# Two transformer layers on one core: Mish products on VectorE, rounding on ScalarE, w2 two feature tiles behind w1

## Chip, cores and metric

The kernel runs on one core of one Trainium2 chip. The metric is the device time of one execution in microseconds (us). The kernel before takes 3567.12 us (median of 3 runs, 3566.23 to 3567.72).

## What is computed

Two layers, each an attention block and a dense block with residuals, both with the same weights in both layers. `x` is 2048 tokens by 512; there are 32 heads of 16; `w1` is 512 x 1792, `w2` is 1792 x 512. The dense block is what the change touches:

```python
h = layernorm(x) @ w1 + b1
sp = log1p(exp(-abs(h))) + where(h > 0, h, 0)
x = x + (h * tanh(sp)) @ w2          # Mish, then the second matrix
```

## The kernel before

**Numbers and splits.** A float32 matmul is made of three matmuls of a faster type (fp32r): an operand is split into a rounded high part and a low part (the rest), and high x high, high x low and low x high are summed in PSUM (`mm3`, lines 176 to 181). So the Mish result is needed twice: `ah`, its rounding, and `al = act - ah`.

**Stages.** For each of the two layers: normalize and multiply by `wqkv`; attention (some 1250 us); `wo`; then the dense block (`mlp`, line 687), some 340 us each time. In the trace's time the dense blocks lie at about 1445 to 1795 us and 3219 to 3560 us.

**The dense block.** Tokens come in 4 chunks `c` of 512, features in 14 tiles `f` of 128. A step of the loop (line 746) is one `(c, f)`. `hid(c, f)` issues 12 matmuls (w1, output tile `h`) and the Mish chain; then the hooks of that step run; then `outp` of the step LAG = 3 back issues 12 matmuls (w2, output tiles `mo`) that add up over all 14 `f` in PSUM: 8 with `ah` as the stationary operand (high and low part of w2 in turn for each of 4 token tiles), then 4 with `al`. After `f` = 13 four additions (line 739) put the result onto the residual `x2`, and free the `mo` banks for the next chunk.

**The Mish chain of one tile** (lines 701 to 717, all 128 x 512): ScalarE `hb` = h + b1; VectorE `he` = min(hb, 10); ScalarE exp; VectorE `he` = (e + 2) e; ScalarE `hr`: a logarithm and an exponential that make the reciprocal; GpSimd `hb` = hb x he (line 708); VectorE `ah` = hb x hr, rounded as it is written (711 or 715); GpSimd the same product again, unrounded (712 or 716); VectorE `al` = hb - ah (713 or 717). The last two tiles of the last layer have VectorE in GpSimd's place. Tiles `hb`, `ah` and `al` have 2 buffers each, `he` and `hr` have 1. For chunks 1 to 3 `ah` and `al` are written in a permuted token order (views `mixed` and `grouped`, runs of 32).

**What else stands in the block.** The first chunk's block also carries the last quarter of the `wo` projection: `outs[3].parts` (hook at step 2) multiplies `num` by `rec` on VectorE (line 655), rounds `oh` on ScalarE (661) and takes `ol` on VectorE (662), all 128 x 2048; four hooks named `quarter` at steps 5, 6, 7 and 8 issue 12 matmuls each (`wo`). The hooks load the later tiles of w1 and w2 (1 MB each, SP queue). `spread` hooks six parts of the next chunk's normalization onto successive steps: statistics, scaling (278), 32 x 32 transposes (283), writes to DRAM in turned order (286), reading back (291), then split on ScalarE and VectorE (294, 295).

**What sets the order.** Matmuls of a layer are chained in program order. Everything else is placed by a list scheduler at build time, by its own estimate of time with the program order as priority; so an engine's order can differ from the order of the text. At run time every engine, and the SP queue, works strictly in the order so fixed. SBUF tiles of 1 MB share 22 slots (`blk`), and a load waits until the slot's last user is done.

Of the kernel before, what the change touches and what calls it, by code (L numbers as in the profile page):

```python
# [9 lines left out]
F32 = mybir.dt.float32  # L10
F32R = mybir.dt.float32r
BF16 = mybir.dt.bfloat16
AF = mybir.ActivationFunctionType
ALU = mybir.AluOpType
# [4 lines left out]
P = 128  # L19
S, D, H, DH, F = 2048, 512, 32, 16, 1792  # L20
NCH = 4
# [3 lines left out]
FT = F // P  # L25
# [21 lines left out]
GSTEPS = NCH * NKT  # L47
STEPS = NG * GSTEPS
HEADS = STEPS * HG
LAG = 3  # L50
MAX_M = (6, 3, 7)
T_BUFS = {"he": 1, "hr": 1}
NBLK = 22
# [15 lines left out]
def kernel(ctx: ExitStack, tc: tile.TileContext, x, wqkv, wo, w1, b1, w2, out):  # L69
    nc = tc.nc  # L70
    x = x[0]
# [37 lines left out]
    def pbank(tag, name):  # L109
        if tag == "s":  # L110
            return banks["s"].tile([P, 512], F32, tag=tag, name=name, bufs=3)
        return ps.tile([P, 512], F32, tag=tag, name=name, bufs=1)

    def t512(tag, name, dt=F32):
        return tmp.tile([P, 512], dt, tag=tag, name=name, bufs=T_BUFS.get(tag, 2))
# [60 lines left out]
    def mm3(acc, pairs, first=True, last=True, pe=lambda ins: ins):  # L176
        n = len(pairs)
        for i, (ah, al, bh, bl) in enumerate(pairs):
            pe(nc.tensor.matmul(acc, ah, bh, start=first and i == 0, stop=False))  # L179
            pe(nc.tensor.matmul(acc, ah, bl, start=False, stop=False))  # L180
            pe(nc.tensor.matmul(acc, al, bh, start=False, stop=last and i == n - 1))  # L181
# [78 lines left out]
    def mixed(t):  # L260
        return t.rearrange("p (j g r) -> p g j r", j=2, r=TR)

    def grouped(t):
        return t.rearrange("p (g j r) -> p g j r", j=2, r=TR)

    def norm_blocks(src, nm, got, key):
        rs, mv = statistics(src, nm)
        yield
        th = b8([P, KT, CW], F32R, f"th{nm}")
        tl = b8([P, KT, CW], F32R, f"tl{nm}")  # L270
        got[key] = (th, tl)
        raw = tl.bitcast(F32)
        turned = dram.tile([D, CW], F32, name=f"nt{nm}")
        for h in range(2):
            xn = tmp.tile([P, 2, D], F32, tag="raw", name=f"xn{nm}{h}", bufs=3)
            for j in range(2):
                t = h + 2 * j
                nc.vector.tensor_scalar(
                    xn[:, j], src[:, t], mv[:, t, 0:1], rs[:, t : t + 1], op0=ALU.subtract, op1=ALU.mult
                )  # L280
            y = tmp.tile([P, D // TR, 2, TR], F32, tag="raw", name=f"y{nm}{h}", bufs=3)
            for j in range(2):
                nc.vector.transpose(y[:, :, j], xn[:, j].rearrange("p (b r) -> p b r", r=TR))
            for a in range(P // TR):
                n0 = h * CW // 2 + a * 2 * TR
                nc.sync.dma_start(
                    turned[:, n0 : n0 + 2 * TR].rearrange("(b q) n -> q b n", q=TR),
                    y[ts(a, TR)].rearrange("q b j r -> q b (j r)"),
                )
            yield  # L290
        nc.sync.dma_start(raw, turned.rearrange("(k p) n -> p k n", p=P))
        yield
        for k in range(KT):
            nc.scalar.activation(th[:, k], raw[:, k], AF.Copy)
            nc.vector.tensor_tensor(tl[:, k], raw[:, k], th[:, k].bitcast(F32), op=ALU.subtract)
            if k % 2:
                yield

    def spread(hooks, c, f0, src, nm, got, key):
        parts = norm_blocks(src, nm, got, key)  # L300
        for i in range(6):
            hooks.setdefault((c, f0 + i), []).append(lambda: next(parts, None))

    class Attention:
# [9 lines left out]
        def pe(self, ins):  # L314
            if self.chained:
                if self.last is not None:
                    tc.add_manual_dep(
                        ins.ins,
                        self.last.ins.name,
                        mybir.DependencyInfo(mybir.DependencyClass.NoSync, mybir.DependencyReason.DATA),  # L320
                        reason="issue order",
                    )
                self.last = ins
# [363 lines left out]
    def mlp(l, x2s, w1t, w2t, tts, dst, hooks, pe):  # L687
        acts, obs = {}, {}

        def hid(c, f):  # L690
            th, tl = tts[c]
            w = w1t[f // 2]
            acc = pbank("s", f"h{l}{c}{f}")
            mm3(
                acc,
                [(w[:, 0, k, ts(f % 2, P)], w[:, 1, k, ts(f % 2, P)], th[:, k, :], tl[:, k, :]) for k in range(KT)],
                pe=pe,
            )
            nm = f"{l}{c}{f}"
            hb, e, r = t512("f", "hb" + nm), t512("he", "he" + nm), t512("hr", "hr" + nm)  # L700
            nc.scalar.activation(hb, acc, AF.Identity, bias=b1t[:, f : f + 1])  # L701
            nc.vector.tensor_scalar(e, hb, HCLAMP, None, op0=ALU.min)  # L702
            nc.scalar.activation(e, e, AF.Exp)  # L703
            nc.vector.scalar_tensor_tensor(e, e, 2.0, e, op0=ALU.add, op1=ALU.mult)  # L704
            nc.scalar.activation(r, e, AF.Ln, bias=1.0, scale=0.5)  # L705
            nc.scalar.activation(r, r, AF.Exp, bias=lnhalf, scale=-1.0)
            mul = nc.vector if (l, c) == (1, NCH - 1) and f >= FT - 2 else nc.gpsimd
            mul.tensor_tensor(hb, hb, e, op=ALU.mult)  # L708
            ah, al = t512("ah", "ah" + nm, F32R), t512("al", "al" + nm, F32R)
            if c:  # L710
                nc.vector.tensor_tensor(mixed(ah), grouped(hb), grouped(r), op=ALU.mult)
                mul.tensor_tensor(hb, hb, r, op=ALU.mult)  # L712
                nc.vector.tensor_tensor(mixed(al), grouped(hb), mixed(ah.bitcast(F32)), op=ALU.subtract)  # L713
            else:
                nc.vector.tensor_tensor(ah, hb, r, op=ALU.mult)
                mul.tensor_tensor(hb, hb, r, op=ALU.mult)
                nc.vector.tensor_tensor(al, hb, ah.bitcast(F32), op=ALU.subtract)
            acts[c, f] = (ah, al)

        def outp(c, f):  # L720
            if f == 0:
                obs[c] = [ps.tile([P, 2, 512], F32, tag="mx", name=f"mo{l}{c}{i}") for i in range(2)]
            ah, al = acts.pop((c, f))
            w = w2t[f // 2]
            for act, parts in ((ah, (0, 1)), (al, (0,))):
                for t in range(NCH):
                    for part in parts:
                        pe(
                            nc.tensor.matmul(  # L729
                                obs[c][t // 2][:, t % 2],  # L730
                                act[:, ts(t, P)],
                                w[:, part, f % 2],
                                start=f == part == 0 and act is ah,
                                stop=f == FT - 1 and act is al,
                            )
                        )
            if f == FT - 1:
                for t in range(NCH):
                    nc.vector.tensor_tensor(x2s[c][:, t], obs[c][t // 2][:, t % 2], x2s[c][:, t], op=ALU.add)
                    if l == 1 and c == NCH - 1:  # L740
                        nc.sync.dma_start(dst[c * CW + t * P : c * CW + (t + 1) * P, :], x2s[c][:, t])
                if l == 0 or c < NCH - 1:
                    nc.sync.dma_start(dst[ts(c, CW), :].rearrange("(t p) d -> p t d", p=P), x2s[c])

        seq = [(c, f) for c in range(NCH) for f in range(FT)]
        for i in range(len(seq) + LAG):
            if i < len(seq):
                c, f = seq[i]
                hid(c, f)
                for fn in hooks.get((c, f), []):  # L750
                    fn()
            if i >= LAG:
                outp(*seq[i - LAG])

# [47 lines left out]
    for l in range(2):  # L802
# [19 lines left out]
        wot, w1t, w2t, x2s, tts = [], [], [], [], {}  # L822
# [13 lines left out]
        hooks = {}  # L836
# [46 lines left out]
        hooks = {}  # L883

        def on(f, fn, c=0):
            hooks.setdefault((c, f), []).append(fn)
# [5 lines left out]
            for _ in range(KT):  # L892
                next(rest)

        for f in range(5, 9):
            on(f, quarter)
        for i, (f1, f2) in enumerate(((0, 0), (2, 2), (4, 6), (7, 8)), 3):
            on(f1, lambda i=i: load_w1(i))
            on(f2, lambda i=i: load_w2(i - 1))
        on(9, lambda: load_w2(6))  # L900
        for c in range(NCH - 1):
            spread(hooks, c, 5 if c else 0, x2s[c + 1], f"m{l}{c + 1}", tts, c + 1)
        wts, tt = {}, {}
        if l == 0:
            last = NCH - 1
# [34 lines left out]
```

## Time and profile before

| | |
|---|---|
| median of 3 runs | 3567.12 us |
| the profiled execution | 3567.44 us |
| its span in the trace | 3565.7 us |
| TensorE (PE) busy | 3524.6 us, 99% |
| VectorE (DVE) busy | 3028.7 us, 85% |
| ScalarE (ACT) busy | 2519.1 us, 71% |
| GpSimd (POOL) busy | 571.0 us, 16% |
| granted TensorE clock, mean | 0.996 |

The span is what the engines' instructions cover; 1.7 us of the execution lie around it. A row of the view by lines reads: line, engine, operation, output tile <- input tiles, shapes, count | busy us, mean ns of one | idle time of the engine just before, and what ended it. A row of the view of time reads: start us, duration us, engine, line, operation, tiles [idle before <- releaser]. A row of waits reads: who waited, for whom, us in total, times, longest. A matmul's row is longer than its share of the time, since matmuls overlap.

### The profile page before, as it was taken

What the parts mean: (1) busy time and instruction counts of PE and PEld (TensorE: products, weight loads), DVE (VectorE), ACT (ScalarE), POOL (GpSimd) and SP (SyncE); (2) the same over time, 40 slices, a digit from 0 to 9 for tenths busy, and PEclk for the clock granted to TensorE, in tenths of its full rate; (3) what the DMA queues carried; (4) which work ended last, traced back from release to release, by engine and by line L of the source; (5) the groups of instructions that cost most, each with busy time, mean ns of one, the idle gap of its engine ahead of it and who ended that gap; (6) DMA issues with size and microseconds to landing.
All of it is one profiled execution on the core that took longest, in us unless ns stands there. A gap on an engine that the chain in (4) does not pass through costs nothing.

```text
span 3565.7 us, 69085 instructions
## 1 busy us (share of the span) xinstructions
PE 3524.6 (99%) x28572; PEld 1931.1 (54%) x28572; DVE 3028.7 (85%) x3052; ACT 2519.1 (71%) x3401; POOL 571.0 (16%) x612
## 2 busy tenths in 40 slices
PE   9999999999999999999999999999999999999999
PEld 7644444444444444777776444444444444447777
DVE  6799999999999994766756999999999999937666
ACT  3288888888888887344422888888888888863444
POOL 3101001000000002455520000000000000024554
PEclk9999999999999999999999999999999999999999
DMA  7641322312222124620364211112121121256000
GB/s 249 225 90 50 79 56 64 62 61 59 66 60 47 52 69 78 224 68 24 107 219 145 47 38 41 35 29 47 29 46 28 41 38 50 61 94 223 36 12 24
DMA packets 182199, 273.99 MB, mean 77 GB/s; under 512 B 67508, under 2 KB 111476, under 8 KB 168060
## 3 DMA queue, kind: packets, MB, share of 16 engines
q1 hardware_dynamic: 154964, 192.91, 21.1%
q10 hardware_dynamic: 19176, 43.06, 3.5%
q0 software_dynamic: 7744, 33.60, 3.3%
q8 instruction: 224, 3.67, 0.4%
q14 instruction: 91, 0.75, 0.1%
HBM read 158.87 MB, written 109.58 MB: 75 GB/s over the span
## 4 chain that ended last, share of the span: by engine, by line
PE 89%; DVE 5%; POOL 2%; ACT 2%; issue 1%; DMA 1%; DVEq 0%; ACTq 0%; POOLq 0%
PE pv L457 30%; PE pm L383 17%; PE ss L441 13%; PE sp L431 9%; PE mo L729 6%; PE qk L179 2%; PE h L179 2%; PE h L181 2%; PE h L180 2%; PE qk L180 1%; PE qk L181 1%; POOL hb L712 1%; DVE al L713 1%; PE wo L179 1%; PE va L179 1%
## 5 line engine op out<-in xcount | busy, mean ns | idle before, releaser
L387 DVE TENSOR_REDUCE mxv<-pm 128x2 f32<-128x1024 f32 x2048 | 2385.3, 1219 | 138.1 <-PE pm L383 89.1
L432 ACT ACTIVATE p<-sp 128x1024 f32<-128x1024 f32 x1366 | 1395.7, 1022 | 18.9 <-PE sp L431 14.6
L457 PE MATMUL pv<-p,va 128*32 128x256 f32 (+2 forms) x16032 | 1167.0, 392 | 0.1
L383 PE MATMUL pm<-ks,qs 48*128 48x512 f32 x4096 | 1097.9, 447 | 0.2
L442 ACT ACTIVATE p<-ss 128x512 f32<-128x512 f32 x1364 | 814.6, 597 | 349.7 <-PE ss L441 272.6
L431 PE MATMUL sp<-qs,ks 50*128 50x512 f32 x2732 | 726.2, 446 | 0.3
L383 PEld LDWEIGHTS pm<-ks,qs 48*128 48x128 f32 x4096 | 451.4, 184 | 345.1 <-issue 177.4
L457 PEld LDWEIGHTS pv<-p,va 128*32 128x32 f32 x16032 | 368.1, 108 | 496.3 <-issue 418.7
L441 PE MATMUL ss<-qs,ks 50*128 50x512 f32 x1364 | 612.5, 449 | 0.0
L441 PEld LDWEIGHTS ss<-qs,ks 50*128 50x128 f32 x1364 | 252.3, 185 | 329.4 <-ACT p L442 225.4
L431 PEld LDWEIGHTS sp<-qs,ks 50*128 50x128 f32 x2732 | 261.6, 183 | 200.2 <-ACT p L432 118.3
L402 POOL CAST np<-nt 128x32 fp32r<-128x32 f32 x64 | 13.3, 208 | 2212.5 <-DVE nt L400 2174.5
L705 ACT ACTIVATE hr<-he 128x512 f32<-128x512 f32 x112 | 70.8, 632 | 215.0 <-POOL hb L712 128.3
L713 DVE TENSOR_TENSOR al<-hb,ah 128x512 fp32r<-128x512 f32 x84 | 122.6, 1459 | 72.4 <-POOL hb L712 70.0
L712 POOL TENSOR_TENSOR hb<-hb,hr 128x512 f32<-128x512 f32 x82 | 139.1, 1696 | 204.0 <-ACT he L703 139.7
L708 POOL TENSOR_TENSOR hb<-hb,he 128x512 f32<-128x512 f32 x110 | 148.7, 1351 | 58.5 <-DVE he L704 55.6
L173 ACT ACTIVATE pt<-qk 128x512 fp32r<-128x512 f32 x64 | 38.2, 597 | 142.2 <-PE qk L181 105.1
L703 ACT ACTIVATE he<-he 128x512 f32<-128x512 f32 x112 | 70.8, 632 | 82.1 <-DVE he L702 72.8
L702 DVE TENSOR_SCALAR he<-hb 128x512 f32<-128x512 f32 x112 | 52.6, 470 | 84.7 <-ACT hb L701 62.7
L701 ACT ACTIVATE hb<-h,b1t 128x512 f32<-128x512 f32 x112 | 76.9, 687 | 64.4 <-DVE al L713 28.4
L704 DVE SCALAR_TENSOR_TENSOR he<-he 128x512 f32<-128x512 f32 x112 | 82.0, 732 | 21.4 <-ACT he L703 14.0
L174 DVE TENSOR_TENSOR pt<-qk,pt 128x512 fp32r<-128x512 f32 x64 | 43.9, 685 | 50.5 <-ACT pt L173 48.3
(240 smaller groups left out, 3186.6 us busy)
## 6 DMA issues: line engine op xcount, KB each, us to landing
scr<-pt ACTq DMA_DIRECT2D x64, 512.0 KB
qs<-scr SPq DMA_DIRECT2D x174, 128.0 KB
ks<-scr SPq DMA_DIRECT2D x174, 128.0 KB
vscr<-v SPq DMA_DIRECT2D x32, 512.0 KB
va<-vscr SPq DMA_DIRECT2D x64, 256.0 KB
oscr<-ot SPq DMA_DIRECT2D x64, 256.0 KB
ww<-sw POOLq DMA_DIRECT2D x14, 1024.0 KB, 5.0
num<-oscr SPq DMA_DIRECT2D x64, 128.0 KB
```

Of the source, the lines that this page charges most:

```text
L179: pe(nc.tensor.matmul(acc, ah, bh, start=first and i == 0, stop=False))
L383: nc.tensor.matmul(pm[:, e], qs[u][rows, q0 : q0 + P], ks[u][rows, ts(n, 512)], start=True, stop=True)
L387: nc.vector.tensor_reduce(self.mxs[b][:, 2 * u : 2 * u + 2, qt, n], pm, axis=AX.X, op=ALU.max)
L431: self.pe(nc.tensor.matmul(sp[:, e], k, q, start=True, stop=True))
L432: nc.scalar.activation(self.pts[-1][:, 0:n], sp[:, 0:n], AF.Exp, scale=SCALE)
L441: self.pe(nc.tensor.matmul(sp, k, q, start=True, stop=True))
L442: nc.scalar.activation(self.pts[i // 3][:, 2], sp, AF.Exp, scale=SCALE)
L457: nc.tensor.matmul(self.accs[b][ts(h, VW), cols], self.va[b // NCH][:, kt, h, :], self.pts[j][:, e, cols], start=kt == 0 and q0 == 0, stop ...
L708: mul.tensor_tensor(hb, hb, e, op=ALU.mult)
L712: mul.tensor_tensor(hb, hb, r, op=ALU.mult)
L713: nc.vector.tensor_tensor(mixed(al), grouped(hb), mixed(ah.bitcast(F32)), op=ALU.subtract)
L729: nc.tensor.matmul(obs[c][t // 2][:, t % 2], act[:, ts(t, P)], w[:, part, f % 2], start=f == part == 0 and act is ah, stop=f == FT - 1 and ...
```

## The change

LAG goes from 3 to 2. Both Mish products are VectorE's, always; the product is taken once, and the rounding of `ah` is a ScalarE copy. Of each `outp` the matmuls with the high part of w2 come first for all four token tiles, then those with the low part, then `al`; for the last feature tile each token tile's three matmuls stand together. The four quarters are hooked at steps 6 to 9, and the next chunk's normalization, for chunk 1, at steps 7 to 12 in place of 0 to 5.

```diff
-LAG = 3
+LAG = 2
...
-            mul = nc.vector if (l, c) == (1, NCH - 1) and f >= FT - 2 else nc.gpsimd
-            mul.tensor_tensor(hb, hb, e, op=ALU.mult)
+            nc.vector.tensor_tensor(hb, hb, e, op=ALU.mult)
+            nc.vector.tensor_tensor(hb, hb, r, op=ALU.mult)
             ah, al = t512("ah", "ah" + nm, F32R), t512("al", "al" + nm, F32R)
-            if c:
-                nc.vector.tensor_tensor(mixed(ah), grouped(hb), grouped(r), op=ALU.mult)
-                mul.tensor_tensor(hb, hb, r, op=ALU.mult)
-                nc.vector.tensor_tensor(mixed(al), grouped(hb), mixed(ah.bitcast(F32)), op=ALU.subtract)
-            else:
-                nc.vector.tensor_tensor(ah, hb, r, op=ALU.mult)
-                mul.tensor_tensor(hb, hb, r, op=ALU.mult)
-                nc.vector.tensor_tensor(al, hb, ah.bitcast(F32), op=ALU.subtract)
+            high, low, full = (mixed(ah), mixed(al), grouped(hb)) if c else (ah, al, hb)
+            nc.scalar.activation(high, full, AF.Copy)
+            nc.vector.tensor_tensor(low, full, high.bitcast(F32), op=ALU.subtract)
             acts[c, f] = (ah, al)
...
-            for act, parts in ((ah, (0, 1)), (al, (0,))):
-                for t in range(NCH):
-                    for part in parts:
-                        pe(
...
+            terms = [[(t, act, part) for t in range(NCH)] for act, part in ((ah, 0), (ah, 1), (al, 0))]
+            turns = zip(*terms) if f == FT - 1 else [terms[0] + terms[1], terms[2]]
+            for t, act, part in (x for turn in turns for x in turn):
+                pe(
...
-        for f in range(5, 9):
+        for f in range(6, 10):
             on(f, quarter)
...
-            spread(hooks, c, 5 if c else 0, x2s[c + 1], f"m{l}{c + 1}", tts, c + 1)
+            spread(hooks, c, 5 if c else 7, x2s[c + 1], f"m{l}{c + 1}", tts, c + 1)
```

In the changed file the same lines lie up to five higher or lower: 707 and 708 are the products, 711 the copy, 712 `al`, 724 the w2 matmuls, 734 the additions; 701 to 706 keep their numbers.

More of the change, by code (lines that the diff above doesn't have):

```diff
@@ L724, in outp @@
             w = w2t[f // 2]
-            for act, parts in ((ah, (0, 1)), (al, (0,))):
-                for t in range(NCH):
-                    for part in parts:
-                        pe(
[L729 to L736, printed above, removed]
+            terms = [[(t, act, part) for t in range(NCH)] for act, part in ((ah, 0), (ah, 1), (al, 0))]
+            turns = zip(*terms) if f == FT - 1 else [terms[0] + terms[1], terms[2]]
+            for t, act, part in (x for turn in turns for x in turn):
+                pe(
+                    nc.tensor.matmul(
+                        obs[c][t // 2][:, t % 2],
+                        act[:, ts(t, P)],
+                        w[:, part, f % 2],
+                        start=f == part == 0 and act is ah,
+                        stop=f == FT - 1 and act is al,
+                    )
+                )
             if f == FT - 1:
```

## The prediction

> **What bounds the kernel now.** I read the page's busy shares first, then TensorE's waits in the two stretches that hold the dense blocks, then the clock in those stretches, then one tile's chain in order of time.
>
> ```profile
> PE 3524.6 (99%) x28572; PEld 1931.1 (54%) x28572; DVE 3028.7 (85%) x3052; ACT 2519.1 (71%) x3401; POOL 571.0 (16%) x612
> ```
>
> TensorE is busy 99% of the span, and the change takes no matmul away. So all that can be won is what TensorE waits, and what its clock loses by waiting. The changed program has the same instructions in the same order outside the dense blocks (on all engines; only names differ), so I look there alone. Waits from 1444.67 to 1800, then from 3218.9 to the end:
>
> ```profile
> PE wo L179 <- ACT oh L661: 6.5, 1, 6.5
> PE mo L729 <- DVE x L739: 6.2, 3, 4.3
> PE mo L729 <- DVE al L713: 1.6, 1, 1.6
> PE wo L181 <- DVE ol L662: 1.2, 1, 1.2
> PE mo L729 <- DVE al L717: 0.6, 2, 0.4
> ...
> PE wo L179 <- ACT oh L661: 6.5, 1, 6.5
> PE mo L729 <- DVE x L739: 3.4, 3, 2.1
> PE wo L181 <- DVE ol L662: 1.2, 1, 1.2
> PE mo L729 <- DVE al L717: 1.0, 2, 0.8
> ```
>
> 16.1 + 12.1 = 28.2 us of idle time in 15 waits. The clock, for the four stretches in which it was halved and one undisturbed stretch of 60 us (columns: stretch, length, busy us and count of PE, PEld, DVE, ACT, POOL, granted clock, DMA share, GB/s):
>
> ```profile
> 1472.10:1482.35 10.25, 6.79 (x15) 4.92 (x16) 8.38 (x11) 4.96 (x6) 5.06 (x3) 0.50 0.74 254
> 1639.36:1646.19 6.83, 5.84 (x14) 4.60 (x15) 6.33 (x15) 2.60 (x4) 3.08 (x3) 0.50 0.41 155
> 3247.04:3257.28 10.24, 7.05 (x16) 5.09 (x17) 8.37 (x11) 4.96 (x6) 5.32 (x3) 0.50 0.75 263
> 3414.29:3417.70 3.41, 3.41 (x9) 2.65 (x10) 2.13 (x4) 1.32 (x2) 0.67 (x1) 0.50 0.79 296
> 1560.00:1620.00 60.00, 60.00 (x261) 48.82 (x261) 41.52 (x59) 28.36 (x45) 31.59 (x22) 1.00 0.19 53
> ```
>
> Undisturbed, 261 matmuls take 60 us: 0.23 each, 2.77 a block of 12, 5.53 a step. At half clock TensorE worked 6.79 + 5.84 + 7.05 + 3.41 = 23.1 us, half of it lost: 11.5. A matmul's row lasts about 0.39 though the next starts after 0.23, so a wait also costs 0.16 more than the idle time shown: 15 x 0.16 = 2.4. **What waiting costs now: 28.2 + 11.5 + 2.4 = 42.1 us.** That is the ceiling, but for the tail.
>
> Why it waits, in one tile of the steady part:
>
> ```profile
> 1700.97 0.69 ACT L701 ACTIVATE hb<-h,b1t 128x512 f32<-128x512 f32 x1 [0.47 <-DVE al L713]
> 1701.77 0.43 DVE L702 TENSOR_SCALAR he<-hb 128x512 f32<-128x512 f32 x1 [0.89 <-ACT hb L701]
> 1702.23 0.63 ACT L703 ACTIVATE he<-he 128x512 f32<-128x512 f32 x1 [0.57 <-DVE he L702]
> 1702.89 0.69 DVE L704 SCALAR_TENSOR_TENSOR he<-he 128x512 f32<-128x512 f32 x1
> 1702.96 1.77 POOL L712 TENSOR_TENSOR hb<-hb,hr 128x512 f32<-128x512 f32 x1 [2.63 <-ACT he L703]
> 1704.77 0.63 ACT L705 ACTIVATE hr<-he 128x512 f32<-128x512 f32 x1 [1.91 <-POOL hb L712]
> 1705.44 0.73 ACT L706 ACTIVATE hr<-hr,lnhalf 128x512 f32<-128x512 f32 x1
> 1707.77 0.69 DVE L711 TENSOR_TENSOR ah<-hb,hr 128x512 fp32r<-128x512 f32 x1
> 1708.62 1.77 POOL L712 TENSOR_TENSOR hb<-hb,hr 128x512 f32<-128x512 f32 x1 [2.63 <-ACT he L703]
> 1710.43 1.77 DVE L713 TENSOR_TENSOR al<-hb,ah 128x512 fp32r<-128x512 f32 x1 [1.18 <-POOL hb L712]
> ```
>
> One tile takes 11.2 us from `hb` to the end of `al`, and the next tile's `hb` starts (row 1) when an `al` is done. The ring of `hb`, `hr`, GpSimd's product and `al` comes round in 5.66 us (that product at 1702.96 and 1708.62): longer than TensorE's step, so it loses a little each step and the additions on `x` come late at a chunk's end.
>
> **The change part by part.**
>
> Prices: the rows show, in turn, a VectorE product, the two kinds of `al`, and a ScalarE copy with rounding.
>
> ```profile
> L712 DVE TENSOR_TENSOR hb<-hb,hr 128x512 f32<-128x512 f32 x2 | 1.4, 687 | 0.0
> L717 DVE TENSOR_TENSOR al<-hb,ah x28: 645/690/1778, 1457.3 to 3322.0; 128x512 fp32r<-128x512 f32 x28
> L713 DVE TENSOR_TENSOR al<-hb,ah x84: 674/1768/1781, 1552.1 to 3557.0; 128x512 fp32r<-128x512 f32 x84
> L294 ACT ACTIVATE thm<-tlm x24: 613/617/632, 1485.2 to 3392.1; 128x512 fp32r<-128x512 f32 x24
> ```
>
> A product on VectorE is 0.69 (row 1). `al` is 0.69 or 1.77 (rows 2 and 3: smallest 0.65 and 0.67, largest 1.78); the long ones run beside a GpSimd product, and after the change GpSimd has none: 0.69. The copy is 0.62 (row 4, the same shape and types). So a step costs VectorE 0.43 + 0.69 + 0.69 + 0.69 + 0.69 = 3.19 us in place of 0.43 + 0.69 + 0.69 + 1.77 = 3.58, and ScalarE 0.69 + 0.63 + 0.63 + 0.73 + 0.62 = 3.30 in place of 2.68: both under 5.53. The chain is hb, min, exp, square, two reciprocal steps, product, copy, `al` = 0.69 + 0.43 + 0.63 + 0.69 + 0.63 + 0.73 + 0.69 + 0.62 + 0.69 = 5.80, with about 0.05 at each of 8 hand-overs 6.2 us. LAG 2 leaves four blocks, 11.1 us. So in the steady part TensorE does not wait, though the cover shrinks by one step. If the VectorE terms stayed at 1.77 the step would be 6.4: a rival below.
>
> The waits on the additions (9.6) and on `al` (3.2) go. The changed order has the additions in two pairs beside the last `outp`, whose token tiles now finish one by one: the first pair can end 2.7 us after that block begins, the second at 5.4 to 6.1; the next chunk's w2 block needs those banks at about 5.5 and 6.0. I leave 0.2 for each of 6 chunk changes: 1.2.
>
> Start of each dense block. This is where the shorter lag costs. The first chunk's start before, in order of time:
>
> ```profile
> 1447.60 0.69 ACT L701 ACTIVATE hb<-h,b1t 128x512 f32<-128x512 f32 x1 [8.29 <-PE h L181]
> 1451.61 0.69 DVE L704 SCALAR_TENSOR_TENSOR he<-he 128x512 f32<-128x512 f32 x1 [0.54 <-ACT he L703]
> 1452.84 0.39 PE L179 MATMUL h<-thm,w11l 128*128 128x512 f32 x1
> 1453.00 0.72 ACT L706 ACTIVATE hr<-hr,lnhalf 128x512 f32<-128x512 f32 x1
> 1454.93 1.82 DVE L278 TENSOR_SCALAR xnm<-x,mvm,rsm 128x512 f32<-128x512 f32 x2
> 1469.05 3.35 DVE L655 TENSOR_TENSOR num<-num,rec 128x2048 f32<-128x2048 f32 x1
> 1472.43 1.91 ACT L661 ACTIVATE oh<-num 128x2048 fp32r<-128x2048 f32 x1 [1.91 <-DVE num L655]
> 1474.45 2.28 DVE L662 TENSOR_TENSOR ol<-num,oh 128x2048 fp32r<-128x2048 f32 x1
> ```
>
> After the change the first w2 block stands at 1452.84, where the fourth `h` block stood (row 3). `hr` of tile 0 ends at 1453.72 (row 4); product and copy bring `ah` at 1455.2. Wait: 2.4. Its `al` stands behind two scalings and a 0.69: 1457.3, wait 0.2.
>
> Then the second wait. In layer 0's changed order VectorE and ScalarE do `num`, `oh` and `ol` before tile 3's product and copy. Walking the order with these prices: tile 3's `h` ends at 1461.2, its `hb` (behind tile 2's copy) at 1463.5, min at 1464.3, scalings to 1465.9, `num` (without GpSimd beside it I take 2.3, as `ol`) to 1468.2, `oh` to 1470.1, then square, transposes, product, `ol` to 1473.1, min of tile 4, product 1474.2, copy 1474.8. TensorE wants that `ah` at 1472.1: wait 2.8. So the 6.5 us in front of the first quarter do not vanish: part turns up one block earlier. The quarter itself, one step later, comes at about 1480, with `oh` and `ol` there: the 13.0 and 2.4 go. In layer 1 the order has tile 3's product and copy ahead of `ol`: the same walk gives 0.3 for `ah` and 0.8 for `al`.
>
> Clock after these waits. Idle times of 2.1 or more (the list above: 6.5, 4.3, 2.1) were followed by half clock, the 1.6 was not. The 2.8 I charge with one shortest stretch, 3.41 at half speed: 1.7; the two of 2.4 (2.2 idle) with half of that each: 0.9. The Trainium skill, "TensorE: Matmul & The Clock Gate", section "Why this matters for your kernels", names idle gaps of more than about 3 us as what drops the clock. By that these waits would cost no clock and the sum would be 3.5 us lower; this trace's 2.1 us did drop it, so I keep the charge.
>
> The next chunk's normalization. Its read-back now stands on the SP queue behind the last two w2 loads, and its slot is freed by the last quarter; ScalarE's split of it stands ahead of tile 10's reciprocal.
>
> ```profile
> 1475.64 0.38 SPq L291 DMA_DIRECT2D tlm<-ntm  x1
> 1485.15 2.20 ACT L294 ACTIVATE thm<-tlm 128x512 fp32r<-128x512 f32 x4 [3.87 <-DMA tlm<-ntm]
> ```
>
> Before, it also followed two 1 MB loads and ScalarE had it 9.5 us after its issue. Issued after the last quarter (call its end 0), it lands at about 10; the splits end at 13, VectorE's part at 15.6, tile 10's copy at 17.2; TensorE wants it at 6 blocks = 16.6. I charge 0.5 in each layer: 1.0. The other moves on that queue (w1 and w2 loads some 4 us earlier, transposed writes) have steps of cover. Between the layers I leave 0.3.
>
> The tail.
>
> ```profile
> 3559.75 2.48 DVE L739 TENSOR_TENSOR x<-mo,x 128x512 f32<-128x512 f32 x4 [2.11 <-PE mo L729]
> ```
>
> The four additions run after the matmuls; token by token only the last stays: 1.3 less. LAG 2 leaves two blocks, 5.5, for the last tile's `ah` of about 5.6, and `al` next: 0.3 more. Net 1.0 less.
>
> The reordering of the other w2 matmuls keeps their number and weight loads; the `al` blocks already change banks at every matmul and keep the pace. Nothing.
>
> **Sum**: remaining 2 x (2.4 + 0.2 + 0.9) + (2.8 + 1.7) + 1.1 + 1.2 + 1.0 + 0.3 = 15.1. Gain 42.1 - 15.1 + 1.0 = 28.0. From the profiled execution's 3567.4 (0.3 above the median): **3539.4 us**.
>
> **Rivals.**
> 1. *The waits move rather than go.* The walk through the first steps may be short: if the read-back lands 5 us later and the `oh` work delays tile 3 by as much in layer 1 as in layer 0, that adds 2 x (5 + 1.7) + (1.7 + 1.7) = 16.8: 3556. For it: ScalarE did wait 3.87 for that DMA. Against: the 9.5 us are measured behind the same two loads.
> 2. *The chain becomes the bound: slower.* VectorE's two-input products could run at 1.77, as `al` often does. Then a step is 0.43 + 0.69 + 3 x 1.77 = 6.4, 0.9 over TensorE's over 112 steps: +101 for the gain lost, about 3640. It decides from a mean of 1.47 for those three. Against: the 687 ns row, and an idle GpSimd. A milder form: strict in-order queues make one tile's round end before the next begins, 5.80 - 0.69 + hand-overs = 5.5 to 5.6; that would be as the old ring, slower only with an extra stop each step. The changed order has at most every second tile so bound in the steady part.
> 3. *The change moves the cover and gains only the chunk ends*: 9.6 + 3.2 + half-clock 4.6 = 17: 3550.
>
> **How the numbers follow.** Forecast (3531 to 3546) 0.68; rival 3 and rival 1 (3546 to 3560) 0.22; under 3531, if no clock falls and the start waits are shorter, 0.03; within 0.2% 0.02; slower, rival 2, 0.05. A measurement of this kernel can tell about 0.2%, 7 us. Range 3530 to 3554: the upper end takes in most of rivals 1 and 3. Faster 0.93, same 0.02, slower 0.05.
>
> **What would show it.** TensorE's waits: none on `oh`, `ol` or the additions above 0.3; a wait of about 2.4 on `ah` at both starts and 2.8 in layer 0 before tile 3's w2 block. `al` rows 0.69 throughout; the steady step 5.55. Wrong it is if VectorE's products show 1.7, if ScalarE waits long for the read-back, or if half-clock stretches stand at other places.

## Result and profile after

The changed kernel takes **3532.86 us** (median of 5 runs, 3531.69 to 3537.39) against 3567.12 before (5 runs, 3566.23 to 3567.79): a ratio of 0.9906, 95% interval 0.9891 to 0.9920. The profiled execution is the median one, 3532.86 us with a span of 3531.1: 34.6 us less than the profiled execution of before. The forecast was 3539.4, with 28.0 won.

First the busy shares on the page of the changed kernel:

```profile
PE 3512.9 (99%) x28572; PEld 1922.5 (54%) x28572; DVE 3002.7 (85%) x3160; ACT 2582.8 (73%) x3513; POOL 239.2 (7%) x392
```

TensorE still has 28572 matmuls and 99%. Its busy time shrank by 11.7 us, mostly matmuls that no longer run at half clock; the rest of the gain is idle time that went. What it still waits for in the two dense blocks, first layer, then second:

```profile
PE mo L724 <- ACT ah L711: 3.6, 2, 2.2
...
PE mo L724 <- ACT ah L711: 2.2, 1, 2.2
PE tpm L256 <- DVE xnm L210: 0.4, 1, 0.4
PE mo L724 <- DVE al L712: 0.3, 1, 0.3
```

28.2 us in 15 waits became 6.1 in 4 (`tpm` belongs to the stage before). Nothing waits for `oh`, `ol` or the additions on `x`. What is left are the first w2 block of each layer (2.2 each) and tile 3, in layer 0 on `ah` (1.4) and in layer 1 on `al` (0.3). The clock around both starts, and in the same undisturbed stretch as before:

```profile
1451.82:1455.23 3.41, 1.25 (x6) 0.72 (x5) 3.08 (x7) 2.50 (x4) 0.42 (x1) 1.00 1.03 239
1455.23:1458.65 3.42, 3.42 (x10) 2.65 (x9) 3.02 (x6) 2.65 (x5) 0.00 (x0) 0.50 1.14 164
...
3206.27:3209.68 3.41, 2.73 (x13) 1.92 (x11) 2.61 (x7) 2.52 (x5) 2.73 (x6) 1.00 1.03 241
3209.68:3213.09 3.41, 1.92 (x8) 1.62 (x9) 3.28 (x6) 2.12 (x5) 0.79 (x1) 1.00 1.07 237
...
1560.00:1620.00 60.00, 60.00 (x261) 48.77 (x260) 37.88 (x61) 38.33 (x61) 0.00 (x0) 1.00 0.10 25
```

One stretch at half clock is left, 3.42 us (row 2), where there were 30.7. In the undisturbed stretch (last row) TensorE's 261 matmuls take 60 us as before; VectorE went from 41.5 to 37.9 there, GpSimd from 31.6 to 0, ScalarE from 28.4 to 38.3.

The rows of `al` over both layers of the changed kernel; then VectorE's rows at the chunk end at which the additions came latest, in the kernel before and in the changed one:

```profile
L712 DVE TENSOR_TENSOR al<-hb,ah x112: 650/692/695, 1455.6 to 3523.1; 128x512 fp32r<-128x512 f32 x112
```

```profile
1634.62 1.77 DVE L713 TENSOR_TENSOR al<-hb,ah 128x512 fp32r<-128x512 f32 x1 [1.18 <-POOL hb L712]
1637.28 0.43 DVE L702 TENSOR_SCALAR he<-hb 128x512 f32<-128x512 f32 x1 [0.89 <-ACT hb L701]
1637.62 0.68 DVE L711 TENSOR_TENSOR ah<-hb,hr 128x512 fp32r<-128x512 f32 x1
1638.40 0.69 DVE L704 SCALAR_TENSOR_TENSOR he<-he 128x512 f32<-128x512 f32 x1
1639.01 2.48 DVE L739 TENSOR_TENSOR x<-mo,x 128x512 f32<-128x512 f32 x4
```

```profile
1621.47 1.28 DVE L734 TENSOR_TENSOR x<-mo,x 128x512 f32<-128x512 f32 x2
1622.67 0.68 DVE L704 SCALAR_TENSOR_TENSOR he<-he 128x512 f32<-128x512 f32 x1
1623.27 1.28 DVE L734 TENSOR_TENSOR x<-mo,x 128x512 f32<-128x512 f32 x2
```

Before, the additions stood on VectorE behind a whole round of the ring: `al` waits for GpSimd's product, `hb` waits for `al`, min waits for `hb`, and only then come the additions, 5.8 us after the chunk's last w2 block (TensorE's next block starts at 1633.18). Now they run inside and just behind the last w2 block (1619.42 to 1622.38), and TensorE's next w2 block starts at 1624.97 without a wait.

### The profile page after: what moved, and what is told of

It reads as the page before. It is cut to its first block, busy times and chain, and to the rows that moved or that the text cites. A ratio compares the mean times of both kernels' runs of the same rounds, so it can differ in the third digit from the quotient of the medians.

```text
span 3531.1 us, 68820 instructions
## 1 busy us (share of the span) xinstructions
PE 3512.9 (99%) x28572; PEld 1922.5 (54%) x28572; DVE 3002.7 (85%) x3160; ACT 2582.8 (73%) x3513; POOL 239.2 (7%) x392
## 4 chain that ended last, share of the span: by engine, by line
PE 96%; DVE 2%; DMA 1%; issue 1%; ACT 0%; POOL 0%; SPq 0%; DVEq 0%; ACTq 0%; POOLq 0%
PE pv L457 30%; PE pm L383 18%; PE ss L441 13%; PE sp L431 10%; PE mo L724 8%; PE h L179 3%; PE h L181 3%; PE h L180 3%; PE qk L179 2%; PE qk L180 1%; PE qk L181 1%; PE wo L179 1%; PE va L179 1%; PE wo L181 1%; PE wo L180 1%
## 5 line engine op out<-in xcount | busy, mean ns | idle before, releaser
L705 ACT ACTIVATE hr<-he 128x512 f32<-128x512 f32 x112 | 70.9, 633 | 82.3 <-DVE he L704 82.3
L708 DVE TENSOR_TENSOR hb<-hb,hr 128x512 f32<-128x512 f32 x112 | 77.2, 689 | 51.0 <-ACT hr L706 49.3
L712 DVE TENSOR_TENSOR al<-hb,ah 128x512 fp32r<-128x512 f32 x112 | 77.2, 690 | 36.8 <-ACT ah L711 33.8
L711 ACT ACTIVATE ah<-hb 128x512 fp32r<-128x512 f32 x112 | 70.5, 629 | 50.7 <-DVE hb L708 40.1
```

The lines of the kernel that those rows point to most:

```text
L708: nc.vector.tensor_tensor(hb, hb, r, op=ALU.mult)
```

## Experiments

Theory A was that two things cost the time before: the quarter of `wo` that waits for `oh` and `ol`, and the ring through GpSimd that makes the additions and `al` late; the lag and the order of w2's matmuls are small. The rivals gave the gain to the order and the lag, or said that waits only move. Each run is compared with runs of the kernel before on its own chip (medians of 3566.4 to 3567.7), so a difference between two of the runs carries up to 1.3 us from their chips.

### e1: the quarters alone

```diff
-for f in range(5, 9):
+for f in range(6, 10):
```

> The kernel before, with only the four quarters of wo hooked one step later (steps 6 to 9). Theory A (gains add up: a late quarter costs its two waits and a half-clock stretch, whatever the rest does): 6.5 + 1.2 us of waits and about 3.3 of clock go in each layer, 22 in all, and 1 to 4 come back elsewhere: 3546 to 3550, no half clock near 1472 and 3247, additions still late at the chunk ends. Rival B (the wait moves to the tile behind): 3556 or more, with a wait of 2 us or more on ah or al in the steps 3 to 6.

Measured: 3560.57 us, ratio 0.9983 (0.9975 to 0.9992): 5.9 won, not 17 to 20. The longest of TensorE's waits, layer 0 and layer 1 (`oh` is 1.0 in layer 1):

```profile
PE mo L729 <- DVE x L739: 8.5, 3, 3.5
PE wo L181 <- DVE ol L662: 1.7, 1, 1.7
PE wo L179 <- ACT oh L661: 1.3, 1, 1.3
...
PE mo L729 <- DVE x L739: 5.7, 3, 3.5
PE wo L181 <- DVE ol L662: 1.6, 1, 1.6
```

The wait on `oh` fell from 6.5 to 1.3 as it should. But the additions cost 8.5 and 5.7 in place of 6.2 and 3.4, with half-clock stretches at the first and third chunk ends of layer 0 and the first of layer 1. Half clock behind the quarter's waits shrank from 10.2 us to 3.4 in each layer, but did not go. The theory that gains add up fell. The rival's time (3556 or more) came true, but not its place: the new waits are at the chunk ends, not at the tile behind the quarter. The reading that fits, with e2 and e6 below: the ring is slower than TensorE's step, the pause in front of the quarter had let it catch up, and without the pause it is later at the chunk ends.

### e2: the Mish products alone

```diff
-            mul.tensor_tensor(hb, hb, e, op=ALU.mult)
+            nc.vector.tensor_tensor(hb, hb, e, op=ALU.mult)
+            nc.vector.tensor_tensor(hb, hb, r, op=ALU.mult)
...
+            nc.scalar.activation(high, full, AF.Copy)
```

> The kernel before, with only the Mish products on VectorE and the rounding on ScalarE (LAG 3, old order of w2, quarters at steps 5 to 8). Theory A (the ring through GpSimd made the chunk ends late, GpSimd beside VectorE made al and num slow): the waits on the additions shrink to under 1 us each, those on al go, half clock at the chunk ends goes (17 us), and num 2.3 in place of 3.35 makes oh some 3 us earlier, which takes 3 to 6 us of the quarter's wait in each layer: 3538 to 3548. Rival B (the order of w2 and the lag set the chunk ends): the six waits on the additions keep over half of their 9.6 us: 3552 to 3562.

Measured: 3542.18 us, ratio 0.9934 (0.9922 to 0.9947): 24.3 won. All waits in the dense blocks:

```profile
PE wo L179 <- ACT oh L661: 4.6, 1, 4.6
PE wo L181 <- DVE ol L662: 1.7, 1, 1.7
...
PE wo L179 <- ACT oh L661: 6.2, 1, 6.2
PE wo L181 <- DVE ol L662: 1.7, 1, 1.7
```

This is theory A's range. Every wait on the additions and on `al` is gone, with LAG 3 and the old order, so they came from GpSimd's part in the ring. Whether the waiting for its products or the slower VectorE rows beside them did more isn't separated here. `oh` came 2.9 us earlier (it starts at 1469.51; before, 1472.43), but TensorE comes sooner too.

### e6: both together

The edits of e1 and e2, nothing else.

> The kernel before with two of the parts: Mish products on VectorE, rounding on ScalarE, and the quarters one step later; LAG 3, old order of w2, old place of the normalization. Theory A (these two are the whole gain; the ring through GpSimd is why the quarters alone gave little): the 14.2 us of waits on oh and ol that the Mish part alone leaves, and its two half-clock stretches, go but for about 2: 3524 to 3530, as the changed kernel with LAG 3. Rival B (order of w2 and the later normalization gave some of it): 3533 or more.

Measured: 3525.17 us (3524.08 to 3527.13), ratio 0.9884 (0.9870 to 0.9897): 41.7 won, where the two alone won 5.9 and 24.3. One wait is left in the two dense blocks together, and no half clock between matmuls:

```profile
PE wo L181 <- DVE ol L662: 0.8, 1, 0.8
```

So two of the change's parts give more than the whole change. The other three together cost 7.7.

### e4 and e12: the lag put back

```diff
-LAG = 2
+LAG = 3
```

> The changed kernel with LAG 3. Theory A: the waits of 2.2 on the first ah of both layers, the 1.4 on tile 3 and the half-clock stretch (1.7) go, 8 us, and the tail stays: 3524 to 3528. Rival B: with two buffers of ah and al, a lag of 3 lets a copy wait on ScalarE for the w2 block two tiles back, the tiles behind it come late, and new waits of 0.2 or more a step appear: 3533 or more.

Measured: 3525.60 us (3524.85 to 3527.22), ratio 0.9886 (0.9872 to 0.9899), 7.3 below the changed kernel. No wait on `ah` is left; `ol` costs 1.2 and 0.4. As e6 and e4 differ by the order of w2 and the place of the normalization, those two together are worth nothing at LAG 3 (0.4 us, inside the noise), and what the other parts cost is the lag.

e12 has LAG 3 and the quarters at steps 7 to 10.

> The changed kernel with LAG 3 and the quarters at steps 7 to 10. Theory A (what is left there is the wait on ol, 1.2 and 0.4): these go, 1.5 to 2 less than with the quarters at 6: 3522 to 3525. Rival B (one step more delays the read-back of the next chunk's normalization, whose slot the last quarter frees): a wait on thm at the first chunk's end, 3526 or more.

Measured: 3524.99 us (3524.07 to 3526.27), ratio 0.9881 (0.9868 to 0.9895): not told apart from e4. The waits on `ol` went, and in their place tile 3's `ah` is late in layer 0:

```profile
PE mo L724 <- ACT ah L711: 1.5, 1, 1.5
PE mo L724 <- DVE al L712: 0.3, 1, 0.3
```

The read-back that the rival feared was in time. e4, e6 and e12 all beat both kernels.

### e10: lag 3 for the first block only

```diff
-            if i >= LAG:
-                outp(*seq[i - LAG])
+            while done < len(seq) and done <= i - (LAG + 1 if i < 4 else LAG):
+                outp(*seq[done])
+                done += 1
```

> The changed kernel, with the first w2 block of a layer one step later (lag 3 there), the next two together, and lag 2 from then on. Theory A (at the starts the lag costs its wait in layer 1 alone; in layer 0 tile 3's ah comes at its own time, set by num, oh and ol, and the wait only moves there): 2 to 4 us less, 3528 to 3531, with a longer wait on tile 3 in layer 0. Rival B (the terms add up): both start waits, the half-clock stretch and the wait on tile 3 go, 7 us, 3525 to 3527.

Measured: 3529.58 us (3528.91 to 3531.78), ratio 0.9895 (0.9881 to 0.9908), 3.3 below the changed kernel: theory A's range, though the two intervals overlap. In the first layer:

```profile
PE mo L724 <- ACT ah L711: 1.8, 1, 1.8
```

Both start waits went, with the half clock; tile 3's wait grew from 1.4 to 1.8 in layer 0, and 1.1 on `ah` appeared in layer 1. But theory A's mechanism isn't borne out: from a block's first matmul to its last of w2, layer 0 is 3.0 us shorter than in the changed kernel and layer 1 is 1.4. Tile 3's `ah` did not keep its own time. VectorE does its product ahead of `ol` here, in the changed kernel behind it (`ol` at 1470.84, product at 1473.38), so `ah` ends 3.3 us earlier, and TensorE is there 3.7 us earlier:

```profile
1470.06 0.65 DVE L708 TENSOR_TENSOR hb<-hb,hr 128x512 f32<-128x512 f32 x1
...
1470.96 2.29 DVE L662 TENSOR_TENSOR ol<-num,oh 128x2048 fp32r<-128x2048 f32 x1
```

So this run does not tell the lag from the order on VectorE that came with it.

### e3: the quarters back at 5 in the changed kernel

> The changed kernel with the quarters back at steps 5 to 8. Theory A': with the products on VectorE oh ends at 1470.5 and ol at 1473.1, and the first quarter would start at 1473.0, so it waits for next to nothing and gives tile 3 the time it lacked (the wait of 1.4 on ah goes): 3531 to 3533. Rival B (the later step is what won the 22 us of the quarters): 3545 or more, with waits on oh of 3 us or more.

Measured: 3531.88 us (3529.77 to 3533.03), ratio 0.9901 (0.9886 to 0.9916): the same as the changed kernel. No wait on `oh` or `ol` appears:

```profile
PE mo L724 <- ACT ah L711: 2.5, 2, 2.2
...
PE mo L724 <- ACT ah L711: 2.2, 1, 2.2
```

With lag 2 a quarter at step 5 has three w2 blocks ahead of it where lag 3 has two, and `oh` is early by the faster products. The wait of 1.4 on tile 3 went, as theory A' had it, but now the clock was halved behind both start waits, where the changed kernel has it in layer 0 alone. The later quarters do nothing in the changed kernel; at LAG 3 they are worth the 17 us between e2 and e6.

### e11: the lag alone

> The kernel before with only LAG 2. Theory A (a tile through GpSimd takes 11.2 us, the lag covers some 10.2 up to the al matmuls): TensorE waits on al in most steps and for 5 us or more at each start: 3580 to 3600. Rival B (the shorter lag costs what it costs with the products on VectorE, some 7 us): 3570 to 3577.

Measured: 3556.53 us (3551.46 to 3556.69), ratio 0.9966 (0.9954 to 0.9979): 11.2 faster, where both theories said slower. The waits in layer 0:

```profile
PE wo L181 <- DVE ol L662: 2.7, 1, 2.7
PE mo L729 <- DVE ah L711: 2.3, 2, 1.4
PE mo L729 <- issue: 1.6, 1, 1.6
PE mo L729 <- DVE al L713: 1.6, 3, 0.6
PE mo L729 <- DVE x L739: 1.3, 1, 1.3
...
PE wo L179 <- ACT oh L661: 1.0, 1, 1.0
```

What the theories expected is there in part: 2.9 and 3.5 us of waits at the two starts (1.6 and 2.2 of them on the first `ah` block, which the view puts down to issue), and waits on `ah` and `al` at three later tiles of layer 0, not in most steps. But the quarter got a w2 block more ahead of it (6.5 on `oh` became 1.0), and the additions cost 1.3 in place of 6.2. VectorE starts them 0.2 to 1.3 us after the chunk's last w2 matmul, where before it was 2.0 to 6.1. Whether the lag itself or the new order on VectorE freed them wasn't separated.

### e7 and e8: the order of w2

e7 is the changed kernel with the old order of w2's matmuls.

> The changed kernel with the old order of w2's matmuls. Theory A (the order matters at the very end alone): 1.0 to 1.5 us more, 3533 to 3536, no waits on the additions over 0.3. Rival B (the token-by-token order is what lets the additions be in time): six waits of 0.5 to 1.5 on the additions, 3537 to 3545.

Measured: 3539.28 us (3536.07 to 3541.50), ratio 0.9923 (0.9910 to 0.9937): 6 more than the changed kernel (their intervals just overlap), inside the rival's range and above theory A's. There is no wait on the additions, so the rival's reason is not there. Between the profiled executions lie 4.9: 0.9 arise before the first dense block, 1.7 in it (tile 3 and others wait longer on `ah`, 6.9 in all), 1.4 in the second (a half-clock stretch), 0.8 behind the last matmul. Only the last is what theory A meant. At LAG 3 the same orders, with the place of the normalization, gave 0.4 between them (e6, e4). The longest of these waits, 3.2 on tile 3, is not a later `ah`: counted from the block's first matmul, `ah` lets TensorE go on at 30.6 us, in the changed kernel at 30.4. TensorE is there 1.5 us earlier, because here the first wait did not halve its clock. Why `ah` is late at three later tiles of layer 0 (0.2, 0.2 and 1.1) stays open.

e8 is the changed kernel with LAG 3 and the products on GpSimd.

> The changed kernel with LAG 3 and the Mish products as before (GpSimd): so order of w2, quarters and normalization of the changed kernel, on the old ring. Theory A (the ring sets the lateness at the chunk ends; the order can't help): 3555 to 3562, waits on the additions of 8 us or more in all. Rival B (the order takes up to 2 us off each of the six waits, and the clock with it): 3540 to 3550.

Measured: 3567.84 us (3565.86 to 3569.21), ratio 1.0002 (0.9994 to 1.0011): no gain over before, and 7.3 slower than e1, from which it differs by the order of w2 and the place of the normalization; above theory A's range. In layer 0:

```profile
PE mo L729 <- DVE x L739: 13.1, 5, 3.0
```

The new order asks for all four token tiles within its first four matmuls, where the old one has two matmuls on each in turn; on the old ring both pairs of additions are waited for, 5 waits in place of 3.

### e5 and e9: work for the idle GpSimd

```diff
+            for _ in range(6):
+                nc.gpsimd.tensor_tensor(idle, idle, idle, op=ALU.mult)
```

> The changed kernel, and GpSimd gets work again that nobody waits for: 6 products of 128 x 192 on a tile of its own beside each Mish tile. Theory A (VectorE's two-input work shares something with GpSimd: al at 1.77 and num at 3.35 in the kernel before are that): al, the products and num show long forms again, the step of VectorE grows from 3.2 towards 5 to 6.4, and the time is 3545 to 3640. Rival B (the long rows came from the ring's own hand-overs, or from the permuted views; GpSimd's work beside costs nothing): al stays at 0.69 and the time at 3531 to 3536.

A miss: with nothing to wait for, all 672 products ran in the first 503 us, none in a dense block. The ten runs spread from 3546 to 4465 us, with mean clocks from 0.998 down to 0.764; in the profiled one 54.6 us outside the dense blocks ran at half clock. So the time isn't used. e9 ties them to their tile by reading `hb`:

```diff
+            for _ in range(6):
+                nc.gpsimd.tensor_tensor(idle, hb[:, 0:192], hb[:, 192:384], op=ALU.mult)
```

> The changed kernel, and GpSimd takes 6 products of 128 x 192 from each finished hb into a tile that nobody reads; unlike those of the run before it, these are tied to their tile and so run inside the dense blocks. Theory A (VectorE's two-input work is slowed by GpSimd's): al and the products show rows well over 0.69 beside them, as al did in the kernel before, the step's 3.2 us of VectorE grow past 4.5, and with only two tiles of lag TensorE waits on ah again: 3545 or more. Rival B (the ring's hand-overs or the permuted views made the long rows): all rows stay at 0.69, 3531 to 3537.

Measured: 3608.90 us (3607.07 to 3610.01), ratio 1.0114 (1.0099 to 1.0130): 76 more than the changed kernel. Smallest, median and largest ns in the dense blocks:

```profile
L712 DVE TENSOR_TENSOR al<-hb,ah x112: 643/917/1092, 1456.9 to 3600.0; 128x512 fp32r<-128x512 f32 x112
...
L704 DVE SCALAR_TENSOR_TENSOR he<-he x112: 643/990/1094, 1451.9 to 3596.0; 128x512 f32<-128x512 f32 x112
...
L710 POOL TENSOR_TENSOR idle<-hb x672: 590/926/2535, 1454.8 to 3603.5; 128x192 f32<-128x192 f32 x168
...
  ACT hb L701: 90.8, 63
```

VectorE's `al` went from 0.69 to 0.92, its square from 0.69 to 0.99, GpSimd's product from 0.51 (e5) to 0.93; ScalarE's 0.63 stayed (median of L705). So the two engines do slow each other, and the permuted views are not the reason (`al` has them here and in the changed kernel). The full 1.77 of before isn't reproduced by these smaller products; in the kernel before, each of the 70 rows of `al` over 1.2 us overlaps a 128 x 512 product of GpSimd by 1.2 us. The Trainium skill, "GPSIMD Engine Reference", section "8. Key points", says that GpSimd shares its SBUF interfaces with VectorE and collides with its two-input instructions; these rows agree. The 76 us are not that price alone: the six products take 5.6 us a tile, as long as TensorE's step, and hold `hb`, for which ScalarE waited 90.8 us (last row).

## Why the prediction was right, and where its sizes were off

- **What bounds the kernel**: right. 42.1 us of waiting was the ceiling; 6.1 idle, 1.7 of clock and 0.6 for 4 waits are left, 8.4. The gain follows: 42.1 - 8.4 and the tail is 34, measured 34.6.
- **Prices**: right. Products and `al` 0.69 (rows 650 to 695), copies 0.63, steady step 5.55 (the prediction reckoned with 5.53; its own row, 261 matmuls in 60 us, gives 5.52). Rival 2 (products at 1.77) did not happen with GpSimd idle; e9 shows that slower products were a real danger with GpSimd at work.
- **Start waits, 2.4 each**: right, 2.2 idle each. Clock after them: 0.9 + 0.9 charged, 1.7 and 0 measured. That the sum fits is luck: the same two waits halved the clock in both layers in e3, and in layer 1 alone in e7.
- **Tile 3 in layer 0, 2.8 + 1.7 of clock**: mis-sized, and the largest miss. The walk said that its `ah` ends at 1474.8 and that TensorE wants it at 1472.1:

```profile
1466.25 2.29 DVE L655 TENSOR_TENSOR num<-num,rec 128x2048 f32<-128x2048 f32 x1
...
1468.62 1.92 ACT L661 ACTIVATE oh<-num 128x2048 fp32r<-128x2048 f32 x1 [2.53 <-DVE num L655]
...
1474.10 0.63 ACT L711 ACTIVATE ah<-hb 128x512 fp32r<-128x512 f32 x1
1474.78 0.96 PE L724 MATMUL mo<-w21l,ah 128*128 128x512 f32 x3 [1.41 <-ACT ah L711]
```

  `ah` ends at 1474.73. But TensorE came there at some 1473.2, slowed by the half clock that the sum had charged apart: waits on a chain of other engines swallow losses ahead of them, and the sum took both. The 1.41 then cost no clock. 4.5 was charged, 1.6 measured. e7 shows the other side of it: VectorE and ScalarE work in the same order there, the clock was not halved before, and the wait on tile 3 is 3.2.
- **Tile 3 in layer 1, 1.1**: 0.3 idle, and about 0.4 more in matmuls around it that start 0.34 to 0.39 apart in place of 0.23.
- **Chunk ends, 1.2, and the read-back, 1.0**: no wait. At the chunk ends the prediction gave a share to the new order of w2; e2 has the old order and no wait either. The read-back had ScalarE start 9.9 us after its issue (forecast 10), and what follows went faster than walked: tile 10's copy ended 15.2 us after the issue (forecast 17.2), and TensorE wanted it at 16.0:

```profile
1508.37 0.39 SPq L291 DMA_DIRECT2D tlm<-ntm  x1
1518.22 2.19 ACT L294 ACTIVATE thm<-tlm 128x512 fp32r<-128x512 f32 x4 [1.88 <-DMA tlm<-ntm]
```

- **The tail, -1.0**: from the last matmul's end to the span's, 5.5 became 4.7; the last w2 block itself takes 0.4 longer.
- **"The shorter lag costs" (as argued from the start waits)**: right with the products on VectorE, 7.3 (e4), and wrong as a general statement: on the old ring the lag of 2 won 11.2 (e11). The prediction never priced the lag apart, on either ring, nor against the quarter, which gets one more w2 block ahead of it.
- **The quarters, 13.0 and 2.4**: the waits went, but not by the step named. e3 shows that the later step is not needed once the products are fast and the lag is 2.

## What to carry to other kernels

Price parts of a change together: here one edit alone won 5.9, another 24.3, both 41.7, because without the second part of what the first saved came back as waits at the chunk ends. Where a wait ends in a chain on other engines that runs at its own time, losses ahead of it come off the wait; do not charge both in full. And before shortening a lag, try it apart: the faster producer made the longer one free, and the version without that part is 7 us better.

## What the runs showed of the hardware

The clock was halved by what fell into fixed stretches of 3.41 us, not by the length of a gap alone. All halvings in a trace lie a whole number of 3.413 us apart (before: 1472.10, 1639.36, 3247.04; 49 and 520 of them from the first). The two starts of the changed kernel have the same gap of 2.2: in layer 0 it lay in one stretch (2.16 idle of 3.41, first rows above) and the next ran at half, in layer 1 it was cut (0.68 and 1.49) and the clock stayed. In e7:

```profile
1471.10:1474.51 3.41, 1.64 (x8) 1.01 (x6) 3.41 (x4) 2.44 (x4) 0.00 (x0) 1.00 0.51 125
1474.51:1477.93 3.42, 1.97 (x9) 1.61 (x10) 3.06 (x6) 3.06 (x5) 0.00 (x0) 1.00 1.00 402
1477.93:1481.34 3.41, 3.41 (x16) 2.80 (x15) 3.11 (x5) 2.59 (x5) 0.00 (x0) 1.00 1.01 428
3211.90:3215.31 3.41, 1.43 (x6) 1.21 (x7) 3.16 (x6) 2.15 (x4) 1.27 (x1) 1.00 1.06 227
3215.31:3218.73 3.42, 3.42 (x9) 2.68 (x9) 2.99 (x6) 3.15 (x6) 0.00 (x0) 0.50 1.14 217
```

A gap of 3.2 cut into 1.77 and 1.45 cost nothing (rows 1 to 3); one of 2.2 with 1.98 in one stretch was followed by half clock (rows 4 and 5). So the same wait is free or costs 1.7 us by where it falls. There is no sharp limit in the idle time as the view shows it. In e1 a stretch with 1.64 idle, made of two shorter waits, was followed by half clock:

```profile
3246.86:3250.28 3.42, 1.78 (x7) 1.15 (x8) 3.42 (x3) 0.43 (x1) 3.19 (x1) 1.00 0.91 237
3250.28:3253.69 3.41, 3.41 (x10) 2.65 (x9) 2.24 (x5) 2.52 (x4) 1.67 (x2) 0.50 0.95 396
```

In the traces of this case, the first stretch of each left out, every stretch at full clock with 1.84 us idle or more was followed by half clock and none with 1.62 or less was; between 1.64 and 1.79 it went both ways, and why stays open. The Trainium skill, "TensorE: Matmul & The Clock Gate", section "Why this matters for your kernels", which the prediction weighed, names gaps over about 3 us; these rows do not bear that out, as a gap of 2.2 halved the clock and one of 3.2 did not.
